# Segment 0 moved into the load phase of a memory-recurrent attention kernel, with batched rows redistributed over the segments

## The chip, the cores and the metric

The kernel runs on one core of one Trainium2 chip. The metric is the device time of an execution in microseconds. Seven runs of the kernel before have a median of 942.41 us (939.52 to 943.75). Below, us are microseconds, PE is TensorE, DVE is VectorE, ACT is ScalarE, POOL is GpSimd, SP is SyncE, which here only issues transfers.

## The reference, cut to what matters

Part A is an attention over segments with a memory: 64 segments of 32 tokens, each preceded by 8 memory rows that are the first 8 output rows of the segment before.

```
for s in range(n_seg):                       # 64 segments, in sequence
    xs = x[:, s*32:(s+1)*32]                 # layer-normed input
    h = concatenate([mem, xs], axis=1)       # 8 + 32 rows
    q, k, v = h@Wq, h@Wk, h@Wv               # 32 heads of 128
    p = softmax(where(mask, q@k.T * scale, -1e9))
    o = (p @ v) @ Wo                         # 40 rows of 512
    mem = o[:, :8];  outs.append(o[:, 8:])
h = x + concatenate(outs)
h2 = h + gmlp(layernorm(h))                  # part B
```

Each segment waits for the one before through `mem`. Of h's 40 rows in a segment, 8 are memory rows and 32 are rows of x, which are known from the start.

## The kernel before, in words

The program is recorded by an `Emitter`: each call of `pe`, `act`, `dve`, `pool`, `sp` appends an instruction to that engine's list, with waits derived from the tokens that it reads and writes. So each engine works in the order in which the Python code calls it, and a call that stands early is executed early on its engine. PE's list is the order of the work. PSUM has 8 banks, which are tokens too.

**What is done per segment and what in batches.** A segment computes 32 of its 40 rows itself: 8 memory rows and the first 24 rows of x (the slot `hT`). The last 8 rows of x of each segment ("x rows" here) are done in batches: a chunk is 16 segments, so 128 rows, gathered by `load_xe`, normalised (`ln_inplace`), transposed (`xT`) and kept in `hTe`. For a chunk, 16 groups `qkx_mm`/`qkx_evac` (L370 to L389; 16 matmuls of 128x128 each, into `QTx`) make their Q and K, and 8 groups `vx_mm`/`vx_evac` (L391 to L410; 16 matmuls on 32 columns with 512 elements each) make their V. V of the batch is staged in the two buffers `Vs`, stored to DRAM (`vext_d`), and read back per segment by `load_vx` (L412) into `Vx`, in another layout. A load of `Vx` needs all 8 groups of its chunk to be stored.

**Load phase (L290 to L709).** SP issues, in order: the rows of chunks 0 and 1, four quarters of Wq, the memory, two blocks of x (which wait until the first buffers are free), four quarters of Wk, of Wv, of Wo, 1 MB each. PE transposes the rows of chunks 0 and 1, does the 16 Q/K groups of chunk 0 (after group 7 it transposes two blocks of x and the memory), then the 8 V groups of chunk 0, and then segment 0. The V groups are stored from ACT's queue. `late_consts` (L303) is a row of 35 small instructions on POOL that builds masks; the reciprocal root of a layer norm (L334, L336) is on POOL too, behind what stands there.

**The loop over segments (L764).** In PE's order: Q and K of both halves (`QK`, L437, 64 matmuls), scores (`S_half`), exponential, V (`V_half`, L531), sums (L497, L502), logarithm (L509), reciprocal by exponential (L513), normalisation on DVE (`sm_norm`, L517, L522), then `PV_half` (L548, L554; the second needs `Vx`), evacuation to `cT` (L567, L569), `Wo` (L581), evacuation to `part` (L593), `mem_out` (L600) and its copy into the next segment's slot (L603), after which the next segment's L437 may begin. Every fourth segment also has `F_group` and `WoX_scatter` (L610, L635) for a finished block of 128 rows, `WoX_mm` (L625) runs in each segment from 4 on.

Into this order are put: one Q/K group of the next chunk in each of segments 0 to 47, between the V matmuls and PV (`gx.pour(16)`, L819), and the V groups of the next chunk in 8 of 16 segments (`VXS`, L745): one atom (4 matmuls) ahead of `Wo`, two ahead of `mem_out`, one behind it (L833, L847, L856). SP issues in each second segment a piece of the transposed w_sp (`wT_piece`, L669: a transposing load, then a store that waits for it).

After the loop stands part B (L876 on), which the change doesn't touch.

Of the kernel before, what the change touches and what calls it, by code (L numbers as in the profile page):

```python
# [33 lines left out]
class Emitter:  # L34
    ENGS = ("pe", "act", "dve", "pool", "sp")

    def __init__(self, n_dma_sems=16):
        self.ops = []
        self.by_eng = {e: [] for e in self.ENGS}
        self.last_w = {}  # L40
        self.readers = {}
        self.n_dma_sems = n_dma_sems
        self.dma_rr = 0
        self.dma_cnt = [0] * n_dma_sems
        self.dma_last = [None] * n_dma_sems
        self.const_tokens = set()
# [4 lines left out]
    def add(self, eng, fn, reads=(), writes=(), dma=False, after=()):  # L51
# [21 lines left out]
        if dma:  # L73
            j = self.dma_rr
            self.dma_rr = (self.dma_rr + 1) % self.n_dma_sems
            op.is_dma = True
            op.dma_sem = j
            self.dma_cnt[j] += 1
            op.dma_val = 16 * self.dma_cnt[j]
            if self.dma_last[j] is not None:  # L80
                deps.add(self.dma_last[j])
            self.dma_last[j] = op
# [78 lines left out]
def fast_path(nc, st, keep, A_x, A_mem0, A_Wq, A_Wk, A_Wv, A_Wo, A_seg_len, B_w_in, B_w_sp, B_b_sp, B_w_out, out):  # L161
# [15 lines left out]
    CK = 16  # L177
# [29 lines left out]
    hTe = sb("hTe", [128, 2, DC, 128], BF)  # L207
# [69 lines left out]
    def load_x(rb, j):  # L277
        sp(lambda e: e.dma_start(xn[:, j, :], xr[:, rb, :]), writes=[("xn", j)])

    def load_xe(ck, j):  # L280
        sp(lambda e: e.dma_start(xn[:, j, :], xe[CK * ck:CK * ck + CK, XM:SEG, :]), writes=[("xn", j)])
# [7 lines left out]

    load_xe(0, 0)  # L290
    load_xe(1, 1)
    for hq in range(4):
        load_w(0, hq)
# [37 lines left out]
    def ln_inplace(j):  # L331
        dve(lambda e: e.bn_stats(out=st1[:, j, :], in_=xn[:, j, :]), reads=[("xn", j)], writes=[("st1", j)])
        dve(lambda e: e.bn_aggr(out=mv1[:, j, :], in_=st1[:, j, :]), reads=[("st1", j)], writes=[("mv1", j)])
        pool(lambda e: e.tensor_scalar(out=rs1[:, j:j + 1], in0=mv1[:, j, 1:2], scalar1=EPS, scalar2=None, op0=ALU.add),  # L334
             reads=[("mv1", j)], writes=[("rs1", j)])
        pool(lambda e: e.tensor_tensor(out=rs1[:, j:j + 1], in0=rs1[:, j:j + 1], in1=mhalf[:, 0:1], op=ALU.pow),  # L336
             reads=[("rs1", j), "mhalf"], writes=[("rs1", j)])
        dve(lambda e: e.tensor_scalar(out=xn[:, j, :], in0=xn[:, j, :], scalar1=mv1[:, j, 0:1], scalar2=rs1[:, j:j + 1],
                                      op0=ALU.subtract, op1=ALU.mult),
            reads=[("xn", j), ("mv1", j), ("rs1", j)], writes=[("xn", j)])  # L340

    def xT(j, bank):
        for dc in range(DC):
            pe(lambda e, dc=dc: e.transpose(out=psb[:, bank, dc * 128:(dc + 1) * 128], in_=xn[:, j, dc * 128:(dc + 1) * 128],
                                            identity=ident[:, :]),
               reads=[("xn", j), "ident"], writes=[PB(bank)])
# [10 lines left out]
    def xe_copy(ck, bank):  # L357
        src = psb[:, bank, 0:512].rearrange("p (dc c) -> p dc c", dc=DC)
        act(lambda e: e.activation(out=hTe[:, ck % 2, :, :], in_=src, func=ACT.Copy), reads=[PB(bank)], writes=[("hTe", ck % 2)])
# [10 lines left out]
    def qkx_mm(ck, i, bank, only_hh=None, only_dc=None):  # L370
        mi, h0 = i // 8, 4 * (i % 8)
        ws = (w_q, w_k)[mi]
        for hh in range(4):
            h = h0 + hh
            for dc in range(DC):
                if only_hh is not None and (hh, dc) != (only_hh, only_dc):
                    continue
                pe(lambda e, h=h, dc=dc, hh=hh: e.matmul(ps[:, bank, hh * 128:(hh + 1) * 128], lhsT=ws[:, dc, h * DH:(h + 1) * DH],  # L378
                                                         rhs=hTe[:, ck % 2, dc, :], start=(dc == 0), stop=(dc == DC - 1)),
                   reads=[("hTe", ck % 2), ("W", mi, h // 8)], writes=[PB(bank)])  # L380
# [10 lines left out]
    def vx_mm(ck, n, bank, only=None):  # L391
        for dc in range(DC):
            if only is not None and dc != only:
                continue
            for c in range(4):
                q = slice(32 * c, 32 * c + 32)
                pe(lambda e, dc=dc, c=c, q=q: e.matmul(ps[q, bank, :], lhsT=hTe[:, ck % 2, dc, q], rhs=w_v[:, dc, n * 512:(n + 1) * 512],  # L397
                                                       start=(dc == 0), stop=(dc == DC - 1), tile_position=(0, 32 * c)),
                   reads=[("hTe", ck % 2), ("W", 2, n // 2)], writes=[PB(bank)])

    def vx_evac(ck, n, bank, eng="act", queue="sp"):
        j = n % 2
        if eng == "act":
            act(lambda e: e.activation(out=Vs[:, j, :], in_=ps[:, bank, :], func=ACT.Copy), reads=[PB(bank)], writes=[("Vs", j)])  # L404
        else:
            dve(lambda e: e.tensor_copy(out=Vs[:, j, :], in_=ps[:, bank, :]), reads=[PB(bank)], writes=[("Vs", j)])
        b, c = n // 4, n % 4
        dst = vext_d[ck, 4 * c:4 * c + 4, :, b * DH:(b + 1) * DH].rearrange("g t e -> t g e")
        em.add(queue, lambda e: e.dma_start(dst, Vs[:, j, :].rearrange("p (g e) -> p g e", g=4)), dma=True, reads=[("Vs", j)],
               writes=[("vext", ck, n)])  # L410

    def load_vx(s):  # L412
        i = s % CK
        sp(lambda e: e.dma_start(Vx[:, s % NVX, :, :], vext_d[s // CK, :, 8 * i:8 * i + 8, :]),
           reads=[("vext", s // CK, n) for n in range(8)], writes=[("Vx", s % NVX)])
# [259 lines left out]
    for j in range(2):  # L675
        ln_inplace(j)
        xT(j, 6 + j)
        xe_copy(j, 6 + j)
    load_x(0, 0)
    load_x(1, 1)  # L680
# [3 lines left out]
    ebank = (0, 1, 2, 3)  # L684

    def start_group(cnt, mm, ev, *a):
        bk = ebank[cnt % 4]
        mm(*a, bk)
        ev(*a, bk, "act" if cnt % 2 == 0 else "dve")

    for i in range(16):
        start_group(i, qkx_mm, qkx_evac, 0, i)
        if i == 7:
            for j in range(2):
                ln_inplace(j)
                xT(j, 6 + j)
                ring_copy(j, 6 + j)
            mem0_transpose(5)
# [6 lines left out]
    for n in range(8):  # L705
        bk = ebank[n % 4]
        vx_mm(0, n, bk)
        vx_evac(0, n, bk, "act" if n % 2 == 0 else "dve", "act")
    for s in range(2):  # L709
        load_vx(s)  # L710
# [20 lines left out]
    gx, gv = Gap(), Gap()  # L731

    def qkx_atoms(ck, i):
        mms = [lambda ck=ck, i=i, hh=hh, dc=dc: qkx_mm(ck, i, XB, hh, dc) for hh in range(4) for dc in range(DC)]
        f = lambda: qkx_evac(ck, i, XB, "dve")
        f.eng = "dve"
        gx.add(XB, mms, f)

    def vx_atoms(ck, n):
        mms = [lambda ck=ck, n=n, dc=dc: vx_mm(ck, n, VXB, dc) for dc in range(DC)]  # L740
        f = lambda: vx_evac(ck, n, VXB, "act")
        f.eng = "act"
        gv.add(VXB, mms, f)

    VXS = (0, 1, 4, 5, 7, 8, 9, 12)  # L745
# [18 lines left out]
    for s in range(NSEG):  # L764
        j4 = s % 4
        rb = s // 4
        ck, i16 = s // CK + 1, s % CK
        if ck < NCK:
            if i16 == 0:
                for n in range(8):  # L770
                    vx_atoms(ck, n)
            qkx_atoms(ck, i16)
# [8 lines left out]
        if i16 == 11 and 2 <= ck + 1 < NCK:  # L781
            load_xe(ck + 1, 1)
# [6 lines left out]
        if s == NSEG - 1:  # L789
            load_wT(0, [lastop["q"]])  # L790
        S_half(s, 0)
        sm_exp(0)
        V_half(s, 0)
# [11 lines left out]
        sm_rcp(0)  # L805
        V_half(s, 1, (0, 1, 2))
# [12 lines left out]
        ev = gx.pour(16)  # L819
        PV_half(s, 0)  # L820
        PV_half(s, 1)
        cT_evac(0, "act")
# [9 lines left out]
        vx = i16 in VXS  # L832
        late = gv.pour(vx)  # L833
# [11 lines left out]
        if i16 == 12 and 2 <= ck + 1 < NCK:  # L845
            ln_inplace(1)
        late += gv.pour(2 * vx)  # L847
# [3 lines left out]
        if i16 == 13 and 2 <= ck + 1 < NCK:  # L851
            xT(1, XB)
            late.append(lambda: xe_copy(ck + 1, XB))
        if s + 1 < NSEG:
            mem_out(s)
        late += gv.pour(vx)  # L856
# [15 lines left out]
    assert not gx.atoms and not gv.atoms  # L872
# [922 lines left out]
```

## Time and profile before

| what | value |
|---|---|
| median of 7 runs | 942.41 us |
| profiled execution, its own time | 942.1 us |
| its span in the trace | 940.4 us |
| PE busy | 882.6 us (94%) |
| DVE, ACT, POOL busy | 445.3, 478.5, 109.0 us |
| chain that ended last | PE 90%, ACT 4%, DVE 2%, DMA 2% |
| first L437 of segment 0 / of segment 1 | 51.37 / 65.19 us |
| last L603 (end of segment 62) | 746.21 us |

How to read it: the span is cut by the profiler at the first and last instruction, the run's own time includes what lies around it. "Busy" of PE is the time in which some matmul is in flight. The chain that ended last is followed back from the last instruction to whatever released each step. The granted clock (PEclk) is the share of full speed that TensorE had. Line numbers are those of the kernel before; after the change they are some 25 higher from L412 on.

### The profile page before, as it was taken

How to read it: one execution, taken by the hardware profiler on the slowest of the kernel's cores; microseconds unless marked ns; L12 is line 12 of the kernel's file. 1: busy time of each engine (PE TensorE's matmuls, PEld its weight loads, DVE VectorE, ACT ScalarE, POOL GpSimd, SP SyncE). 2: the span in 40 equal slices, each digit the busy share in tenths (PEclk: the TensorE clock that was granted, in tenths of full speed). 3: DMA queues.
4: the chain of work that ended last, by engine and by line, in shares of the span. 5: the costliest groups of instructions: out<-in, count | busy, mean ns of one | idle time of the engine just before them, and what ended most of it. 6: DMA issues, size and time to landing. Idle time of an engine off the chain costs nothing.

```text
span 940.4 us, 45489 instructions
## 1 busy us (share of the span) xinstructions
PE 882.6 (94%) x20973; PEld 492.2 (52%) x20973; DVE 445.3 (47%) x1029; ACT 478.5 (51%) x1158; POOL 109.0 (12%) x274
## 2 busy tenths in 40 slices
PE   4789999999999999999999999989899999989998
PEld 4545555555555555555555555445444444434443
DVE  3135445455555445555545455444434463453433
ACT  2146666666666666666666666665556565500000
POOL 5001011011111111111111011111101022200000
PEclk9779999999999999999999999999999999999999
DMA  9942012130222222221212131513122193021201
GB/s 333 376 119 69 17 37 65 49 82 20 63 55 56 46 63 45 46 60 38 60 37 66 43 82 23 113 40 68 48 43 63 43 286 106 1 90 45 90 12 36
DMA packets 103668, 71.29 MB, mean 76 GB/s; under 512 B 62248, under 2 KB 89008, under 8 KB 103472
## 3 DMA queue, kind: packets, MB, share of 16 engines
q1 hardware_dynamic: 99248, 67.27, 25.4%
q8 instruction: 166, 2.72, 1.2%
q10 hardware_dynamic: 4224, 1.05, 0.5%
q14 instruction: 30, 0.25, 0.1%
HBM read 39.46 MB, written 18.61 MB: 62 GB/s over the span
## 4 chain that ended last, share of the span: by engine, by line
PE 90%; ACT 4%; DVE 2%; DMA 2%; issue 2%; POOL 0%; ACTq 0%; POOLq 0%
PE f_ps L437 25%; PE f_ps L581 12%; PE f_ps L531 11%; PE f_ps L938 10%; PE f_ps L378 7%; PE f_ps L625 4%; PE f_ps L900 3%; PE f_ps L548 3%; PE f_ps L931 2%; PE f_ps L1008 2%; PE f_ps L397 2%; PE f_ps L600 2%; PE f_ps L476 2%; DMA vext_d<-f_Vs 2%; ACT f_hT L603 1%
## 5 line engine op out<-in xcount | busy, mean ns | idle before, releaser
L437 PE MATMUL f_ps<-f_arena,f_hT 128*32 128x512 bf16 x4096 | 235.5, 383 | 17.3 <-ACT f_hT L603 12.0
L444 ACT ACTIVATE f_Tst<-f_ps 128x512 bf16<-128x512 f32 x256 | 152.6, 597 | 103.4 <-PE f_ps L437 101.2
L437 PEld LDWEIGHTS f_ps<-f_arena,f_hT 128*32 128x32 bf16 x4096 | 104.5, 97 | 127.9 <-ACT f_hT L603 24.1
L531 PE MATMUL f_ps<-f_arena,f_hT 128*32 128x512 bf16 x2048 | 140.2, 378 | 0.0
L450 DVE STREAM_TRANSPOSE f_QT<-f_Tst 128x256 uint32<-128x256 uint32 x128 | 57.0, 446 | 173.8 <-ACT f_Tst L444 173.8
L581 PE MATMUL f_ps<-f_arena,f_cT 128*32 128x384 bf16 (+1 forms) x4096 | 123.6, 273 | 2.1 <-ACT f_cT L567 1.5
L581 PEld LDWEIGHTS f_ps<-f_arena,f_cT 128*32 128x32 bf16 x4096 | 84.8, 97 | 55.9 <-ACT f_cT L567 26.4
L938 PE MATMUL f_ps<-f_arena 128*128 128x512 bf16 x448 | 101.3, 379 | 2.4 <-DVE f_arena L944 1.6
L593 ACT ACTIVATE f_part<-f_ps 128x384 bf16<-128x384 f32 (+1 forms) x128 | 46.4, 384 | 75.1 <-PE f_ps L581 75.1
L453 DVE STREAM_TRANSPOSE f_KT<-f_Tst 128x256 uint32<-128x256 uint32 x128 | 57.0, 445 | 52.7 <-ACT f_Tst L444 52.6
L460 POOL COPY f_QT<-f_arena 128x256 bf16<-128x256 bf16 x64 | 30.8, 481 | 392.7 <-PE f_ps L482 392.6
L569 DVE TENSOR_SCALAR f_cT<-f_ps 128x320 bf16<-128x320 f32 x128 | 56.9, 486 | 38.1 <-PE f_ps L554 38.1
L938 PEld LDWEIGHTS f_ps<-f_arena 128*128 128x128 bf16 x448 | 43.5, 98 | 55.9 <-DVE f_arena L944 2.6
L378 PE MATMUL f_ps<-f_hTe,f_arena 128*128 128x128 bf16 x1024 | 70.3, 227 | 0.1
L378 PEld LDWEIGHTS f_ps<-f_hTe,f_arena 128*128 128x128 bf16 x1024 | 61.7, 102 | 11.7 <-issue 11.6
L567 ACT ACTIVATE f_cT<-f_ps 128x320 bf16<-128x320 f32 x128 | 49.0, 435 | 34.2 <-PE f_ps L554 34.2
L517 DVE SCALAR_TENSOR_TENSOR f_E_sb<-f_R_sb,f_E_sb 128x160 bf16<-128x160 f32 x128 | 41.7, 325 | 46.5 <-ACT f_R_sb L513 46.5
L509 ACT ACTIVATE f_R_sb<-f_ps 128x160 f32<-128x160 f32 x128 | 39.0, 305 | 35.7 <-PE f_ps L502 35.7
L531 PEld LDWEIGHTS f_ps<-f_arena,f_hT 128*32 128x32 bf16 x2048 | 44.6, 95 | 21.0
L589 POOL COPY f_cTx<-f_cT 128x256 bf16<-128x256 bf16 x64 | 26.2, 410 | 196.5 <-DVE f_cT L569 196.5
L397 PE MATMUL f_ps<-f_arena,f_hTe 128*32 128x512 bf16 x512 | 42.2, 394 | 5.0 <-ACT f_Vs L404 4.9
L944 DVE TENSOR_TENSOR f_arena<-f_ps,f_arena 128x512 f32<-128x512 f32 x28 | 19.3, 691 | 57.8 <-PE f_ps L938 57.8
(95 smaller groups left out, 1083.7 us busy)
## 6 DMA issues: line engine op xcount, KB each, us to landing
wT_d<-f_wst SPq DMA_DIRECT2D x32, 256.0 KB, 2.6
f_arena<-wT_d SPq DMA_DIRECT2D x32, 256.0 KB, 4.7
f_arena<-in_A_Wq_dram SPq DMA_DIRECT2D x4, 1024.0 KB, 9.7
f_arena<-in_A_Wk_dram SPq DMA_DIRECT2D x4, 1024.0 KB, 14.1
f_arena<-in_A_Wv_dram SPq DMA_DIRECT2D x4, 1024.0 KB, 14.4
f_arena<-in_A_Wo_dram SPq DMA_DIRECT2D x4, 1024.0 KB, 14.0
f_Vx<-vext_d SPq DMA_DIRECT2D x64, 64.0 KB, 2.9
vext_d<-f_Vs SPq DMA_DIRECT2D x24, 128.0 KB, 2.0
```

Of the source, the lines that this page charges most:

```text
L378: pe(lambda e, h=h, dc=dc, hh=hh: e.matmul(ps[:, bank, hh * 128:(hh + 1) * 128], lhsT=ws[:, dc, h * DH:(h + 1) * DH], rhs=hTe[:, ck % 2, d ...
L397: pe(lambda e, dc=dc, c=c, q=q: e.matmul(ps[q, bank, :], lhsT=hTe[:, ck % 2, dc, q], rhs=w_v[:, dc, n * 512:(n + 1) * 512], start=(dc == 0 ...
L437: pe(lambda e, dc=dc, c=c, rhs=rhs: e.matmul(ps[32 * c:32 * c + 32, bank, :], lhsT=hT[:, sl, dc, :], rhs=rhs, start=(dc == 0), stop=(dc == ...
L444: act(lambda e: e.activation(out=Tst[:, tb, :].rearrange("p (hp i r) -> p hp i r", i=32, r=2), in_=ps[:, bank, :].rearrange("p (hp r i) -> ...
L450: dve(lambda e: e.transpose(out=dst, in_=src), reads=[("T", tb)], writes=[("QT", b)])
L453: dve(lambda e: e.transpose(out=dst, in_=src), reads=[("T", tb)], writes=[("KT", b)])
L531: pe(lambda e, dc=dc, c=c, c0=c0: e.matmul(ps[32 * c:32 * c + 32, bank, :], lhsT=hT[:, sl, dc, :], rhs=w_v[:, dc, c0:c0 + 512], start=(dc ...
L567: act(lambda e: e.activation(out=dst, in_=src, func=ACT.Copy, scale=UNSC), reads=[PB(PVB[c])], writes=[("cT", c)])
L569: dve(lambda e: e.tensor_scalar(out=dst, in0=src, scalar1=UNSC, scalar2=None, op0=ALU.mult), reads=[PB(PVB[c])], writes=[("cT", c)])
L581: pe(lambda e, h=h, g=g, i=i, b=b, c=c: e.matmul(ps[32 * g:32 * g + 32, bank, 0:d1 - d0], lhsT=cTh[:, i, 8:40], rhs=w_o[:, h, d0:d1], star ...
L593: act(lambda e: e.activation(out=part[:, s % 8, d0:d1], in_=ps[:, bank, 0:d1 - d0], func=ACT.Copy), reads=[PB(bank)], writes=[("part", s % ...
L938: pe(lambda e: e.matmul(ps[:, bank, 0:TB], lhsT=z2[:, sc, fb * 128:(fb + 1) * 128], rhs=wTb[tb % 2][:, :, sc, :], start=(sc == 0), stop=(s ...
```

## The change

1. **Loads.** SP issues: rows of chunk 0, Wq's first quarter, rows of chunk 1, two blocks of x, Wq's second quarter, rows of chunk 2, the rest. The two blocks and the rows of chunk 2 go into tiles of `part` (numbers 4, 5, 6), which are free at that time, instead of waiting for `xn`. `hTe` has three buffers instead of two.
2. **Load phase on PE.** Only chunk 0's rows are normalised and transposed ahead of the first Q/K group. The other four are interleaved with groups 1 to 7. After groups 9, 11, 13 and 15 stands one Q/K group of chunk 1 each.
3. **Segment 0** begins after the Q/K groups. The 8 V groups of chunk 0 and four more Q/K groups of chunk 1 stand inside it. Each V group of chunk 0 is staged in a tile of `part` of its own, `Vs` serves the others in turn.
4. **The Vx loads of segments 0 and 1** are issued by POOL, with two semaphores of their own, after `qx_copy(1)`; before, SP issued them ahead of all other transfers of the loop.
5. **In the loop**, `gx` holds one whole group per segment: the 8 V groups of chunk 1 in segments 0 to 7, then the remaining 8 Q/K groups of chunk 1, then those of chunks 2 and 3. The V groups of chunks 2 and 3 are poured one atom behind `mem_out` in each segment and one ahead of it in segments with s mod 4 of 0 or 1, until they are used up (64 atoms, segments 0 to 42). None stands ahead of `Wo`.

```diff
-    hTe = sb("hTe", [128, 2, DC, 128], BF)
+    hTe = sb("hTe", [128, 3, DC, 128], BF)
...
+    def xbuf(j):
+        return (xn[:, j, :], [("xn", j)]) if j < 2 else (part[:, j, :], [("part", j, 0), ("part", j, 1)])
...
     load_xe(0, 0)
+    load_w(0, 0)
     load_xe(1, 1)
-    for hq in range(4):
+    load_x(0, 4)
+    load_x(1, 5)
+    load_w(0, 1)
+    load_xe(2, 6)
+    for hq in range(2, 4):
         load_w(0, hq)
...
     def vx_evac(ck, n, bank, eng="act", queue="sp"):
-        j = n % 2
+        if ck == 0:
+            t, tok = part[:, n, :], [("part", n, 0), ("part", n, 1)]
+        else:
+            j = vcnt[0] % 2
+            vcnt[0] += 1
+            t, tok = Vs[:, j, :], [("Vs", j)]
...
-    for j in range(2):
-        ln_inplace(j)
-        xT(j, 6 + j)
-        xe_copy(j, 6 + j)
-    load_x(0, 0)
-    load_x(1, 1)
+    ln_inplace(0)
+    xT(0, 6)
+    xe_copy(0, 6)
     for hq in range(4):
         load_w(1, hq)
     late_consts()
-    ebank = (0, 1, 2, 3)
+    ebank = (2, 3, 4, 5)
...
     for i in range(16):
-        start_group(i, qkx_mm, qkx_evac, 0, i)
+        start_x(0, i)
+        if i == 1:
+            ln_inplace(1)
+            ln_inplace(4)
+        if i == 3:
+            xT(1, 7)
+            xe_copy(1, 7)
+            ln_inplace(5)
+            ln_inplace(6)
+        if i == 5:
+            xT(4, 6)
+            ring_copy(0, 6)
+            xT(5, 7)
+            ring_copy(1, 7)
         if i == 7:
-            for j in range(2):
-                ln_inplace(j)
-                xT(j, 6 + j)
-                ring_copy(j, 6 + j)
-            mem0_transpose(5)
+            xT(6, 6)
+            xe_copy(2, 6)
+            mem0_transpose(7)
+        if i >= 9 and i % 2 == 1:
+            start_x(1, i // 2 - 4)
...
-    for n in range(8):
-        bk = ebank[n % 4]
-        vx_mm(0, n, bk)
-        vx_evac(0, n, bk, "act" if n % 2 == 0 else "dve", "act")
-    for s in range(2):
-        load_vx(s)
...
+    for n in range(8):
+        vx_group(1, n)
+    for ck, i0 in ((1, 8), (2, 0), (3, 0)):
+        for i in range(i0, 16):
+            qkx_group(ck, i)
+    for ck in (2, 3):
+        for n in range(8):
+            vx_atoms(ck, n)
...
                 QK_evac(s, b, mi)
...
+        if s == 0:
+            for n in range(2):
+                start_v(n)
         S_half(s, 0)
         sm_exp(0)
+        if s == 0:
+            for n in range(2, 4):
+                start_v(n)
+            start_x(1, 4)
         V_half(s, 0)
...
         sm_rcp(0)
+        if s == 0:
+            for n in range(4, 6):
+                start_v(n)
+            start_x(1, 5)
+            for n in range(6, 8):
+                start_v(n)
         V_half(s, 1, (0, 1, 2))
...
-        ev = gx.pour(16)
+        if s == 0:
+            for j in range(2):
+                load_vx(j, "pool")
+        ev = [gx.pop(0)()] if gx else []
         PV_half(s, 0)
         PV_half(s, 1)
+        if s == 0:
+            for i in range(6, 8):
+                start_x(1, i)
         cT_evac(0, "act")
...
-        vx = i16 in VXS
-        late = gv.pour(vx)
+        late = []
         Wo((0, 2, 1, 3), OB, 0, OC)
...
-        late += gv.pour(2 * vx)
+        if j4 < 2:
+            late += gv.pour(1)
...
         if s + 1 < NSEG:
             mem_out(s)
-        late += gv.pour(vx)
+        late += gv.pour(1)
```

## The prediction

> **What bounds the kernel now.** I read the slices of the page first, then the chain of work that ended last for the start, the busy time by stages, and the same chain for single segments of the steady loop. All of it says: TensorE's order of work sets the end, with a hole at the start.
>
> ```profile
> PEclk9779999999999999999999999999999999999999
> ```
>
> A slice is 23.5 us. In slices 2 and 3 TensorE gets 0.7 of its clock, after that the full one to the end. The chain of the start (start, duration, what):
>
> ```profile
> 35.49 7.81 DMA vext_d<-f_Vs
> 43.39 0.61 ACT f_Vs L404
> 44.02 6.62 DMA vext_d<-f_Vs
> 50.72 0.61 ACT f_Vs L404
> 51.37 3.63 PE f_ps L437 x32
> ```
>
> The reader sees that the batched V rows of chunk 0 have only two staging buffers (Vs), so the third group waits 7.8 us until a store has landed, the fifth 6.6 us more. Segment 0 (its L437) starts at 51.37; the same chain has segment 1's L437 at 65.19. The stages (us, PE busy, PEld, DVE, ACT, POOL, granted clock, DMA share, GB/s):
>
> ```profile
> 23.00:29.00 6.00, 5.72 (x55) 5.51 (x56) 0.92 (x2) 1.18 (x3) 0.08 (x1) 0.50 1.05 387
> 39.00:44.00 5.00, 0.13 (x4) 0.00 (x0) 0.00 (x0) 0.60 (x1) 0.00 (x0) 0.90 1.12 359
> 44.00:57.00 13.00, 9.40 (x92) 2.96 (x96) 2.27 (x4) 2.02 (x4) 0.00 (x0) 0.52 0.73 216
> ```
>
> TensorE idles twice for about 5 us: from 17.8 to 23.3 but for four transposes (0.4 us), and from 39.2 to 44.0. After each its clock stands at 0.50, for about 7 and 13 us. DMA, over 1 in its column, is saturated until about 50.7 us (by stretches of 2 us, 48 to 50 has 1.14, 50 to 52 has 0.37): weights fill it.
>
> Now the steady loop. A segment with a Q/K group of the batched rows (L378) and one without, from the chain:
>
> ```profile
> 175.27 0.21 ACT f_hT L603
> ...
> 181.64 1.00 PE f_ps L378 x16
> ...
> 186.24 0.21 ACT f_hT L603
> ```
>
> ```profile
> 669.83 0.21 ACT f_hT L603
> ...
> 676.04 0.31 ACT f_R_sb L509
> 676.37 0.35 ACT f_R_sb L513
> ...
> 680.74 0.21 ACT f_hT L603
> ```
>
> With the group a segment lasts 10.97 us (186.24 - 175.27), without it 10.91 (680.74 - 669.83): its 1.00 us stands in a hole in which TensorE otherwise waits for logarithm, exponential and normalisation. Batched work in the loop is thus nearly free, and moving it out brings nearly nothing. The exception, a V group on a segment that also has F_group and WoX_scatter:
>
> ```profile
> 141.28 0.22 PE f_ps L610 x4
> 141.50 0.21 PE f_ps L635 x4
> 141.71 0.43 PE f_ps L397 x7
> ...
> 142.33 0.21 ACT f_hT L603
> ```
>
> This segment began at 130.91, so it took 11.42: two fillers of 0.43 each ahead of mem_out don't both fit.
>
> **The change, part by part.** The sum is made against the profiled execution, 942.1 us (span 940.4, 1.7 around it); the median of the runs shown is 942.41, 0.3 above.
>
> *Q/K rows in the load phase.* SP now issues xe0, Wq, xe1, x0, x1 and xe2 without its old wait for the transposes (1.6 us on L278, with DMA full anyway: worth nothing). xe2 adds 128 KB, 0.34 us at 387 GB/s. Four layer norms (blocks 1, 4, 5, 6) are interleaved with groups 1 to 7. Their reciprocal root runs on POOL, behind late_consts: that took from 7.61 to 18.89, 11.3 us; it now starts after one norm, at 5.3, and ends at 16.6. So norm 1 is done at 17.9 (0.9 POOL, 0.4 DVE), and each further one takes 2.3 us (18.46 to 20.77 in the trace): 20.2, evacuation of group 3 on DVE 0.7, then 23.2 and 25.5. TensorE runs in order: after group 3 (about 13.4) it stands at the transpose of block 1 until 17.9, a new idle stretch of 4.5 us. From 26.2 there are 12 groups (8 of chunk 0, 4 of chunk 1) at 0.89 us (the spacing of evacuations from 30.3 to 33.9): segment 0 starts at about 36.9. All Wk has landed by then (last issue 12.99 + 15.5 us to landing, + 0.34 = 28.8). If the idle stretch halves the clock, as the two of before did, it is about 39.5.
>
> *Segment 0 with the V groups in it.* Ahead of its PV stand QK 3.64, eight V groups at 0.87, two Q/K groups at 0.9, V 1.73, scores and sums 0.85, a V group of chunk 1 0.87, and a last wait of 0.8 for the normalisation: 16.6 us, so TensorE is at PV at 53.5 (56.1 with the slow clock). The part tiles give all eight V groups a buffer of their own: the 16.8 and 15.1 us of waits of ACT and DVE for stores go.
>
> *What is late next.* PV needs Vx, Vx needs all eight stores, and these share the DMA engines with Wo. Before, DMA was full until 50.7 with four stores served. Queue q10 (the eight stores) took 7.5% of the engines over 62 us, 0.58 us a store. Four more stores 2.3, xe2 0.34, and wT_piece(0), which SP now issues before the Vx loads rather than after, about 1.4 (256 KB in and out at 387 GB/s): full until 54.7 in all, against the last issue of a store at 51.6 + 2 (its landing time once Wo is out). With the landing the last store is in at about 55.5 (before: 57.7, when SP was released). The stores on ACT's queue cost 8 issues of 0.37 us among ACT's segment work; it hides beside TensorE's V groups.
>
> *The Vx loads on POOL.* No transfer is issued by POOL in the trace. Nearest row below: the same load from SP, 2.2 to 2.9 us to landing. Above: the wait of a 128 KB store behind full rings, 7.8. I take 3.2, by the nearer row (same load, DMA nearly empty): Vx is there at 58.7. The second load waits for the first, and cTx_copy(0) behind it on POOL for both; its first waiter is cT_evac of segment 1, some 8 us later: hidden. For a POOL-issued transfer the Trainium skill ("DMA: Bandwidth & Descriptors", Latency and other measured facts) states about 1 us to the first byte against 0.6 from SP; by that the load would take 0.4 more than SP's, 3.3 at most, and no run here shows it.
>
> *After PV.* Two more Q/K groups (1.8 us) stand ahead of Wo. Their evacuations (0.6 ACT, 0.7 DVE) come before cT_evac on both engines, so Wo's later quarters wait: 0.4 PV, 0.9 + 0.7 to the first two evacuations, 0.9 and 1.0 cT, 1.1 rest of Wo, 0.6 part_evac, 0.5 mem_out and hT: 6.0 us, where before took 3.8 (61.42 to 65.19). Segment 1 starts at 58.7 + 6.0 = 64.7, against 65.19: **-0.5 us**. The 14 us that segment 0 starts earlier are given back, as DMA and not TensorE now sets its middle.
>
> *The clock.* TensorE idles at PV from 53.5 to 58.7, 5 us, as long as the stretch from 39.2 to 44.0 after which the clock halved. That would cost half of some 5 us at half speed, 2.5. In the branch with the slow clock earlier the idle is only 3 us. I count +0.2 for the two together. The Trainium skill ("TensorE: Matmul & The Clock Gate", Part 1) speaks against this change: one idle window of 3.4 us halves the clock; by that rule alone the full 2.5 would stand here, and the forecast would be 2.3 later. The rows agree in kind, but the stretch from 47.8 to 51.4 fell in an already slow clock and can't tell the bound.
>
> *Steady loop.* First L603 of the loop at 64.94, last at 746.21, 62 periods; the last 15 are 10.91. So the 47 before average (681.27 - 163.65)/47 = 11.01. After the change a V group of chunk 1 takes the place of a Q/K group in segments 0 to 7 (same hole, 0.87 for 1.00), and a V atom of 0.22 stands behind mem_out in every segment to 42 (in the 0.27 us hole until hT is there) and one ahead of it where no F_group or transpose stands. No segment then carries 0.86 there, which removes three times 0.45, and the rest goes from 10.99 to about 10.96: 47 x 0.05 = **-2.4 us**. Bounds: 0 and 47 x 0.10 = -4.7.
>
> Sum: 942.1 - 0.5 + 0.2 - 2.4 = **939.4 us**.
>
> **Rivals.** *Overlap works better* (0.17): stores drain early, POOL's load lands in 2.2 us, no clock loss: segment 1 at 62 to 62.7, -2.8, steady -2.7: 936.6. For it: DMA has room from 50.7 on. Against: the eight stores' bytes.
> *The clock halves at PV* (0.20): segment 1 at 66.5, +1.3, steady -2.4: 941.0. For it: both idle stretches of 5 us did so.
> *Fillers pay* (0.08): the atom behind mem_out hides a longer hole than 0.27 in all 43 segments, 0.1 more each: 935. Against: segments with and without V groups differ by 0.04 now.
> *Slower* (0.10): the Vx load on POOL comes late. wT_piece(0)'s transpose and store, now ahead, fill the rings, the last store lands 3.9 later (half of the 7.8 above) at 59.4, POOL's load takes 6 (between 2.9 and 7.8), and the clock halves: 59.4 + 6 + 6.0 + 2.5 = 73.9, 8.7 later, less 2.4: 948. For a time 2.8 above the median segment 1 must start 5.5 later, at 70.7: this decides once Vx lands after 64.7, or after 62.2 with the slow clock. Against: SP's own loads there landed in 2.9.
> That the change doesn't do what it says is excluded in part: the order of instructions puts segment 0's L437 before all V groups, but segment 1 may still start no earlier, which is the second rival.
>
> **Numbers.** Forecast 0.45, half of it on either side of 0.3% (2.8 us, about what a measurement of this kernel can tell from no change). Faster: 0.23 + 0.17 + 0.08 = 0.48; within: 0.22 + 0.17 + 0.03 = 0.42; slower: 0.03 + 0.07 = 0.10. The range leaves out the slow case and most of the filler case: 935.5 to 943.0. The forecast's own range is 938 to 941.
>
> **What would show it.** Right: the first wait for POOL in front of the transpose of block 1; L437 of segment 0 near 37 to 39; a wait of TensorE in PV for Vx's DMA, ended near 59; segment 1 at 64 to 65; segments near 10.96. Wrong: segment 1 before 62 (DMA backlog smaller) or after 67 (POOL's load, clock), or periods of 11.0 or more.

## The result and the profile after

| | before | after |
|---|---|---|
| median of all runs | 941.12 us (50 runs, 939.22 to 944.31) | 944.29 us (19 runs, 942.39 to 946.86) |
| profiled execution, its own time | 942.1 us | 943.16 us |
| its span | 940.4 us | 941.4 us |
| first QK matmul of segment 0 | 51.37 us | 36.95 us |
| first QK matmul of segment 1 | 65.19 us | 68.19 us |
| first to last copy into the next slot (62 periods) | 681.3 us | 679.3 us |
| last copy to the end of the span | 194.2 us | 194.2 us |

The changed kernel is slower: its time is 1.0034 of before's, interval 1.0025 to 1.0043, so some 3.2 us. The pair of profiled executions differs by 1.06 us only: 3.0 us lost at the start, 2.0 won in the loop. The rest is in the executions that were profiled: before's lay 1.0 above its median, after's 1.1 below. A second profile of each (the last two experiments) shows where.

In after's code QK is L462, the batched Q/K groups L396, the batched V groups L415, their copies L427 (ACT) and L429 (DVE), PV L573 and L579, Wo L606, the copy into the next slot L628, the Vx load L439.

The slices of after, clock and DMA. The low clock of before's slices 2 and 3 is gone from this coarse view; what is left of it lies within the first and third slice:

```profile
PEclk8989999999999999999999999999999999999999
DMA  9951312140312111221303120413112193021201
```

The chain of after from the last V groups of chunk 0 to segment 1 (start, duration, what):

```profile
49.46 1.87 PE f_ps L415 x32
...
51.36 0.69 DVE f_part L429
52.05 0.12 DVE f_E_sb L542
52.17 5.43 DMA vext_d<-f_part
57.60 0.03 POOLq L154
57.63 0.55 issue
58.18 2.29 DMA f_Vx<-vext_d
...
61.01 3.54 PE f_ps L396 x32
...
64.57 0.69 DVE f_arena L407
65.26 0.41 DVE f_cT L594
...
65.71 1.61 PE f_ps L606 x56
...
67.94 0.21 ACT f_hT L628
...
68.19 1.90 PE f_ps L462 x29
```

Three things are to be read. The last store is issued at 52.2 and has landed at 57.6. POOL then needs 0.55 us to issue the load and 2.29 until it has landed. Behind PV stand two Q/K groups that take 3.54 us for 32 matmuls, twice their usual time, and Wo's later quarters can't run before the evacuations of these two groups.

The same stretch by stages of after (us, busy PE, PEld, DVE, ACT, POOL, granted clock, DMA share, GB/s):

```profile
18.00:22.00 4.00, 3.77 (x36) 3.77 (x37) 2.75 (x7) 1.19 (x2) 0.88 (x3) 0.50 1.05 388
...
48.00:50.00 2.00, 2.00 (x36) 1.27 (x32) 0.68 (x2) 0.60 (x1) 0.00 (x0) 1.00 1.13 358
50.00:52.00 2.00, 2.00 (x51) 0.94 (x40) 0.84 (x3) 0.60 (x1) 0.00 (x0) 1.00 1.77 251
...
58.00:60.00 2.00, 0.00 (x0) 0.00 (x0) 0.00 (x0) 0.00 (x0) 0.77 (x1) 0.53 0.43 137
60.00:62.00 2.00, 1.48 (x35) 1.41 (x36) 0.00 (x0) 0.00 (x0) 0.53 (x1) 0.50 0.03 8
62.00:64.00 2.00, 2.00 (x21) 2.00 (x20) 0.00 (x0) 1.14 (x3) 0.00 (x0) 0.50 0.13 33
```

From 58.1 to 65.0 the clock is halved, just when TensorE has work again. And DMA: its share adds up the times of all packets, so it can pass 1. From 50 to 52 it is 1.77 for 251 GB/s, where the 2 us before have 1.13 for 358, so a byte takes 2.2 times as long. That is when the transposing load of SP's piece of w_sp has come to its turn (its packets run from 50.3 to 54.3).

What TensorE waited for in the start of after (total, times, longest):

```profile
PE f_ps L579 <- DMA f_Vx<-vext_d: 6.3, 1, 6.3
PE f_ps L362 <- DVE f_xn L356: 3.6, 1, 3.6
```

In the loop, the segment of after that has both a V group and F_group and WoX_scatter (L635, L660), from copy to copy:

```profile
133.44 0.21 ACT f_hT L628
...
139.81 0.86 PE f_ps L415 x16
...
143.90 0.22 PE f_ps L635 x4
144.12 0.21 PE f_ps L660 x3
...
144.54 0.21 ACT f_hT L628
```

It took 11.10 us, where the segment of before that the prediction quotes took 11.42: the V group now stands ahead of PV, and only F_group and WoX_scatter lie ahead of `mem_out`.

### The profile page after: what moved, and what is told of

Read it like the earlier page. It is cut to its first block, busy times and chain, and to the rows that moved or that the text cites. A ratio compares the mean times of both kernels' runs of the same rounds, so it can differ in the third digit from the quotient of the medians.

```text
span 941.4 us, 45485 instructions
## 1 busy us (share of the span) xinstructions
PE 889.1 (94%) x20973; PEld 491.1 (52%) x20973; DVE 447.1 (47%) x1033; ACT 475.8 (51%) x1154; POOL 109.9 (12%) x276
## 4 chain that ended last, share of the span: by engine, by line
PE 90%; ACT 3%; DVE 2%; issue 2%; POOL 1%; DMA 1%; POOLq 0%
PE f_ps L462 25%; PE f_ps L606 12%; PE f_ps L556 11%; PE f_ps L1004 10%; PE f_ps L396 6%; PE f_ps L650 4%; PE f_ps L966 3%; PE f_ps L573 3%; PE f_ps L997 2%; PE f_ps L1074 2%; PE f_ps L625 2%; PE f_ps L415 2%; PE f_ps L501 2%; ACT f_hT L628 1%; PE f_ps L522 1%
## 5 line engine op out<-in xcount | busy, mean ns | idle before, releaser
L462 PE MATMUL f_ps<-f_arena,f_hT 128*32 128x512 bf16 x4096 | 232.8, 380 | 9.5 <-ACT f_hT L628 6.4
L462 PEld LDWEIGHTS f_ps<-f_arena,f_hT 128*32 128x32 bf16 x4096 | 104.9, 97 | 120.5 <-ACT f_hT L628 24.1
L606 PE MATMUL f_ps<-f_arena,f_cT 128*32 128x384 bf16 (+1 forms) x4096 | 124.1, 273 | 2.2 <-ACT f_cT L592 1.6
L606 PEld LDWEIGHTS f_ps<-f_arena,f_cT 128*32 128x32 bf16 x4096 | 83.9, 97 | 60.5 <-ACT f_cT L592 30.7
L396 PE MATMUL f_ps<-f_hTe,f_arena 128*128 128x128 bf16 x1024 | 71.7, 230 | 1.6 <-DMA f_arena<-in_A_Wq_dram 1.6
L396 PEld LDWEIGHTS f_ps<-f_hTe,f_arena 128*128 128x128 bf16 x1024 | 63.3, 104 | 12.7 <-issue 9.5
L573 PE MATMUL f_ps<-f_E_sb,f_V_sb 32*128 32x40 bf16 x2048 | 36.8, 178 | 11.1 <-DVE f_E_sb L547 8.9
L1010 DVE TENSOR_TENSOR f_arena<-f_ps,f_arena 128x512 f32<-128x512 f32 x28 | 19.3, 690 | 57.8 <-PE f_ps L1004 57.8
```

The source lines that it names most:

```text
L462: pe(lambda e, dc=dc, c=c, rhs=rhs: e.matmul(ps[32 * c:32 * c + 32, bank, :], lhsT=hT[:, sl, dc, :], rhs=rhs, start=(dc == 0), stop=(dc == ...
L573: pe(lambda e, q=q, c=c, g=g, c0=c0: e.matmul(ps[:, PVB[c], c0:c0 + 40], lhsT=V_sb[q, b, g * 128:(g + 1) * 128], rhs=E_sb[q, b, g * 40:(g ...
L606: pe(lambda e, h=h, g=g, i=i, b=b, c=c: e.matmul(ps[32 * g:32 * g + 32, bank, 0:d1 - d0], lhsT=cTh[:, i, 8:40], rhs=w_o[:, h, d0:d1], star ...
```

## The experiments

**Theory A**, after the first look: the start of after is set by DMA. The last V store lands late behind Wo and the w_sp piece, then come the load of Vx, the two Q/K groups, and most of it at half the clock since TensorE idled for 6.3 us at PV. Its rivals, each in its run: POOL's path for the load; the row of constants on POOL; TensorE's order; the new pattern in the loop.

In the table, "ratio" is against before on the same chip, and the rest is from each kernel's profiled execution (us; an empty cell was not read out): the first QK matmul of segment 0, the last V store landed, Vx there, segment 1's QK in the chain, the half clock near PV (from the trace's record of the clock), the 62 periods of the loop.

| run | median (runs) | ratio, interval | QK 0 | store | Vx | QK 1 | half clock | loop |
|---|---|---|---|---|---|---|---|---|
| after | 944.29 (19) | 1.0034, 1.0025 to 1.0043 | 36.95 | 57.6 | 60.5 | 68.19 | 58.1 to 65.0 | 679.3 |
| after, again | 943.60 (1) | | | 57.1 | 60.1 | 67.83 | 57.4 to 64.3 | 679.0 |
| before, again | 939.88 (1) | | 49.80 | | | 63.88 | 41.4 to 55.1 | 681.0 |
| w_sp piece later | 941.93 (12) | 1.0008, 0.9996 to 1.0020 | 36.9 | 54.9 | 57.9 | 65.19 | 57.6 to 61.0 | 679.2 |
| fillers ahead of PV | 942.06 (12) | 1.0015, 1.0003 to 1.0027 | 37.0 | 56.8 | 59.7 | 65.38 | 58.9 to 65.8 | 679.6 |
| constants later | 943.00 (12) | 1.0023, 1.0012 to 1.0035 | 34.1 | 55.7 | 58.7 | 66.45 | 53.3 to 63.5 | 679.2 |
| old V pattern | 947.35 (6) | 1.0067, 1.0049 to 1.0084 | 36.9 | 57.8 | 60.7 | 70.56 | 56.0 to 69.6 | 681.0 |
| Vx on SP, w_sp later | 941.32 (12) | 0.9991, 0.9979 to 1.0002 | 36.8 | 55.3 | 57.6 | 65.3 | 55.7 to 62.6 | 679.4 |
| before with 8 staging tiles | 938.30 (6) | 0.9959, 0.9942 to 0.9975 | 41.08 | 53.9 | 56.2 | 62.50 | 55.3 to 62.1 | 681.5 |
| w_sp later, fillers ahead | 940.21 (12) | 0.9982, 0.9970 to 0.9993 | | 55.0 | 57.9 | 63.58 | 57.5 to 64.3 | |
| clock kept | 943.75 (12) | 1.0020, 1.0006 to 1.0033 | | 57.1 | 60.0 | 66.01 | none | |
| V first | 942.26 (12) | 1.0002, 0.9989 to 1.0015 | 43.9 | | | 65.79 | 49.6 to 56.4 | 678.9 |
| V first, constants later | 938.52 (10) | 0.9970, 0.9953 to 0.9986 | 41.58 | | | 60.89 | none | 679.2 |

**1. The w_sp piece later.** After with one edit: the first piece goes to segment 1, behind the Vx loads on SP's queue.

```diff
-        if s % 2 == 0 and s // 2 < NWT:
+        if s % 2 == 0 and 0 < s // 2 < NWT:
             wT_piece(s // 2)
+        if s == 1:
+            wT_piece(0)
```

> One part undone: the first piece of the transposed w_sp (a transposing load and a store of 256 KB) is issued by SP in segment 1 instead of ahead of segment 0. Theory A (the start is set by the DMA engines: loads, then eight stores, then the Vx load, and TensorE waits at PV): the last V store lands about 2 us earlier, near 55.5 in place of 57.6, Vx near 58.4 in place of 60.5, segment 1 starts near 66.0 in place of 68.2, time 2 us under the changed kernel. Rival B (the piece is hidden, the stores are late because their packets are slow): stores and segment 1 within 0.5 us of where they were.

The chain of this run:

```profile
51.98 2.90 DMA vext_d<-f_part
...
55.47 2.40 DMA f_Vx<-vext_d
...
65.19 3.64 PE f_ps L462 x64
```

The last store waits 2.90 us instead of 5.43, with its issue at the same time, and segment 1 starts 3.0 us earlier; by the ratios the time falls by 2.4 us (0.0026 of 941). The same piece stands ahead in five profiles (after twice, fillers, old pattern, clock kept: landed at 56.8 to 57.8, mean 57.3) and behind in three (this one, Vx on SP, both together: 54.9 to 55.3, mean 55.1). So it costs the last store 2.2 us, 1.5 to 2.9. (In "constants later" the piece is ahead as well, but the store is issued 3 us earlier.) Of the 3.0 us of segment 1, 2.6 are the earlier Vx and 0.4 the half clock, which was shorter in this profile.

**2. The fillers ahead of PV.** After with the two Q/K groups moved from behind PV to ahead of it, so that they run while Vx is awaited.

```diff
-        PV_half(s, 0)
-        PV_half(s, 1)
         if s == 0:
             for i in range(6, 8):
                 start_x(1, i)
+        PV_half(s, 0)
+        PV_half(s, 1)
```

> The last two Q/K groups of segment 0 stand ahead of PV instead of behind it; nothing else is moved. Theory A: TensorE is idle there anyway (54 to 60.5), so the groups cost nothing in that place, and behind PV the 3.6 us that they took at half clock and the delay of their evacuations go: segment 1 starts 2.5 to 3.5 us earlier, near 65, whether the clock still halves or not; time 2.5 to 3.5 us under the changed kernel. Rival (the two groups were beside other waits behind PV): less than 1 us.

Its chain:

```profile
52.42 4.36 DMA vext_d<-f_part
...
60.75 3.61 PE f_ps L606 x64
...
65.38 3.72 PE f_ps L462 x34
```

From Vx (59.72) to segment 1 it is 5.7 us instead of 7.7, so the two groups cost 2.0 behind PV, and nothing ahead of it. In time it is 1.8 us by the ratios, less than the 2.5 to 3.5 expected; their intervals overlap a little. The clock was halved all the same: Wo's 64 matmuls took 3.61 us, 1.92 in the steady loop.

**3. The constants later.** After with POOL's row of 35 instructions behind the layer norms.

```diff
-    late_consts()
...
             mem0_transpose(7)
+            late_consts()
```

> The row of mask constants on POOL is recorded behind the layer norms of the load phase, so the norms no longer wait for it. The stall of TensorE at the transpose of block 1 (14.5 to 18.2) goes and segment 0 starts near 32 in place of 37. Theory A (DMA sets the start): the V stores are issued 5 us earlier but share the engines with Wo for longer, the last one lands within 1.5 us of 57.6, segment 1 starts within 2 us of 68.2, no gain. Rival D (the stall behind the constants sets the start): segment 1 starts 4 to 5 us earlier, time 4 to 5 us under the changed kernel.

The last store in its chain:

```profile
49.07 6.65 DMA vext_d<-f_part
```

Segment 0 starts 2.9 us earlier (5 were expected), segment 1 only 1.7. After has 52.17 and 5.43 in this line: the store is issued 3.1 us earlier and lands 1.9 earlier. So of what TensorE wins, the part that DMA lets through arrives; in time it is 1.0 us by the ratios, whose intervals overlap, and the 4 to 5 us of the rival are not there.

**4. The old V pattern in the loop.** After with `VXS` and its pours of before for the V groups of chunks 2 and 3 (the V groups of chunk 1 stay ahead of PV).

```diff
+    VXS = (0, 1, 4, 5, 7, 8, 9, 12)
...
-        late = []
+        vx = s % CK in VXS
+        late = gv.pour(vx)
...
-        if j4 < 2:
-            late += gv.pour(1)
+        late += gv.pour(2 * vx)
...
-        late += gv.pour(1)
+        late += gv.pour(vx)
```

> Startup as changed, but the V atoms of chunks 2 and 3 are poured in the old pattern (8 of 16 segments, one atom ahead of Wo, two ahead of mem_out, one behind). My theory of the loop: the even spread is worth about 2 us from segment 1 to the end; with the old pattern the stretch from segment 1 to the end is about 1 to 1.5 us longer than in the changed kernel (16 segments instead of the former 24 carry groups, two of them with 0.45 too much), the start is the same. Rival (the spread itself costs time and the old pattern was better): 1 us or more shorter.

The loop takes 681.0 us, 1.7 more than after's profile and as much as before's. So the spread of the V groups makes nearly all of the 2.0 us that the loop gained. That the start is 2.4 us longer as well was not expected: one V atom then stands ahead of segment 0's Wo, and the clock stayed halved for 13.7 us. How much of the 2.4 is the atom and how much the clock was not separated.

**5. The Vx loads on SP.** Experiment 1 with `load_vx(j)` in place of `load_vx(j, "pool")`.

> As the kernel with the w_sp piece issued in segment 1, and the Vx loads of segments 0 and 1 issued by SP instead of POOL. Theory A: the load from POOL took 2.4 us after 0.55 us until its issue; from SP the same load took 2.2 to 2.9 in the kernel before, so Vx lands within 0.6 us of 57.9 and the time is within 1 us of that kernel. Rival C (the load on POOL is the slow step): segment 1 starts 2 us or more earlier.

The load of this run, from the wait's end to its landing:

```profile
55.31 0.02 issue
55.33 2.25 DMA f_Vx<-vext_d
```

On SP it is 2.3 us, on POOL (experiment 1) 0.03 + 0.55 + 2.40, so 3.0: POOL's path costs 0.7 us (the 0.4 that the prediction quotes for it is too little). But the two profiles reach segment 1 within 0.1 us of each other, as here the store landed 0.4 later and the clock was halved for longer. The ratios, 1.0008 and 0.9991, have intervals that overlap. The load on POOL is not what made the change slow.

**6. Before with eight staging tiles.** The kernel before, in which the V groups of chunk 0 get a tile of `part` each; nothing else of the change.

```diff
+        t, tok = Vs[:, j, :], [("Vs", j)]
+        if ck == 0:
+            t, tok = part[:, n, :], [("part", n, 0), ("part", n, 1)]
...
```

The copies and the store behind it use `t` and `tok` in place of `Vs`.

> The kernel before, with one edit alone: each V group of chunk 0 gets a staging tile of its own (part). The V groups run from 34 to 41 without waiting for stores and segment 0 starts near 41 instead of 51.4. Theory A (the engines of DMA, not the staging, hold the start): the last store lands near 54 instead of 57.7, Vx near 57, TensorE waits 7 us at PV and its clock halves; segment 1 starts near 62.5, 2 to 3 us earlier than in the kernel before, time 2 to 3 us under it. Rival E (staging was the gate): segment 1 starts near 55, time 9 to 10 us under the kernel before.

Its chain (L440 is QK here):

```profile
43.75 10.12 DMA vext_d<-f_part
...
53.88 2.33 DMA f_Vx<-vext_d
...
62.50 3.64 PE f_ps L440 x64
```

This is the kernel with the lowest median of the study: 0.9959 of before, and 0.9925 of after if the two ratios are divided (0.9959 / 1.0034). It has none of the early segment 0 and none of the new loop (681.5 us), yet segment 1 starts at 62.50, 5.7 us before after's. The V groups stand ahead of segment 0, so their stores are queued while Wo still flows; the last one waits 10 us, but beside segment 0's work, and has landed at 53.9. The rival, with segment 1 at 55, fell: a transfer again ends the wait. At PV TensorE waits 2.9 us for it, not the 7 expected, since it has stood 2.4 us earlier for ACT, which was held in the issue of the stores (up to 2.06 us for one).

**7. Both edits, 1 and 2, in one kernel.**

> The changed kernel with both mends: the w_sp piece in segment 1, and the last two Q/K groups ahead of PV. Theory A: Vx near 57.9, TensorE idle for 2.5 to 3 us only, so its clock mostly stays full; segment 1 starts near 62, time 5 to 7 us under the changed kernel and 2 to 4 us under the kernel before. Rival (each mend takes away the same wait): no more than 3 us under the changed kernel.

Segment 1 at 63.58, 4.6 us earlier than after; 4.9 us by the ratios. One by one the two edits brought segment 1 forward by 3.0 and 2.8 (0.8 of the second was a store that landed earlier in that profile), so they nearly add up. The half clock stays, from 57.5, though TensorE waits only 2.7 us for Vx (55.26 to 57.96), and segment 1 misses the expected 62. With these two moves the change makes the kernel a little faster than before (interval 0.9970 to 0.9993).

**8. The clock kept.** After with 96 more matmuls (a Q/K group six times) ahead of PV in segment 0, into a bank whose content is not used, to keep TensorE busy while it waits.

```diff
+        if s == 0:
+            for _ in range(6):
+                qkx_mm(1, 6, 4)
         PV_half(s, 0)
```

> The changed kernel with 96 matmuls more: six times the matmuls of one Q/K group, into a bank that nobody reads in between, ahead of PV of segment 0, where TensorE waits for Vx. The output is the same. Theory A: they fit into the wait (5.4 of 6.4 us), the clock stays full, and the groups and Wo behind PV run at full speed: segment 1 starts 1.5 to 2.5 us earlier than in the changed kernel, near 66, time 1.5 to 2.5 us under it although more is computed. Rival (the clock has no part in it): no gain, or up to 1 us more.

Its chain, and a stage behind PV:

```profile
57.63 2.36 DMA f_Vx<-vext_d
...
60.46 1.91 PE f_ps L396 x32
...
66.01 2.99 PE f_ps L462 x51
```

```profile
60.00:62.00 2.00, 1.96 (x53) 1.92 (x54) 0.00 (x0) 0.50 (x2) 0.53 (x1) 1.00 0.13 33
```

The same 32 matmuls take 1.91 us instead of 3.54, with more work on TensorE and Vx as late as ever (59.99). From Vx to segment 1 it is 6.0 us, in after 7.7: the half clock costs 1.7 us there. In time it is 1.3 by the ratios, whose intervals overlap at their ends; the point rests on the profile.

**9. V first.** After with the V groups ahead of segment 0 as in before, the four Q/K groups of chunk 1 ahead of PV, the w_sp piece later and Vx on SP.

```diff
+    for n in range(8):
+        start_v(n)
...
+        if s == 0:
+            for i in range(4, 8):
+                start_x(1, i)
         ev = [gx.pop(0)()] if gx else []
...
```

The calls of `start_v` and `start_x` that after has inside segment 0 are taken out; the w_sp piece and the Vx loads stand as in experiments 1 and 5.

> Meant to beat both kernels. The changed kernel with: the eight V groups of chunk 0 ahead of segment 0 again (with their eight staging tiles), the four remaining Q/K groups of chunk 1 ahead of PV of segment 0, the w_sp piece in segment 1, the Vx loads on SP. Theory A: V stores issued from 38 to 45, the last lands near 54.5 (DMA full until then, as in the staged kernel before), Vx near 57; TensorE is busy until about 55, so its clock stays full; segment 1 starts near 61, and the loop keeps the 1.8 us of the even spread: time 5 to 6 us under the kernel before (ratio 0.994 to 0.995) and 2 us under the staged kernel before. Rival: the load phase of the change costs what the spread gives, ratio 0.996 as for the staged kernel before.

Neither came out: the time is that of before. Its chain, then two of its stages:

```profile
44.83 1.32 ACTq L432
...
46.82 1.74 ACTq L432
...
48.60 1.66 ACTq L432
...
50.30 1.09 ACT f_Tst L469 x2
```

```profile
48.00:50.00 2.00, 0.00 (x0) 0.00 (x0) 0.00 (x0) 0.00 (x0) 0.00 (x0) 0.89 1.14 362
50.00:52.00 2.00, 0.45 (x12) 0.19 (x16) 0.89 (x2) 1.61 (x4) 0.00 (x0) 0.50 1.16 346
```

TensorE no longer waits for Vx. But ACT, which issues the stores (L432), stands up to 1.74 us in one issue while DMA is saturated, so its first evacuation of segment 0's Q/K comes at 50.30; TensorE waits 3.4 us for it at the scores, and the clock halves. So V first alone brings nothing here: experiment 7, with the V groups inside segment 0, is if anything faster (0.9982 against 1.0002; the intervals just overlap).

**10. V first, constants later.** Experiment 9 with the edit of experiment 3.

> The same with the mask constants behind the layer norms, so the V groups begin 3 us earlier. Theory A (DMA holds Vx): the last store lands within 1 us of the run without this edit, and the time is within 1 us of it. Rival D (the norms hold the start): 2 to 3 us less.

```profile
25.02 14.70 DMA f_arena<-in_A_Wv_dram
...
39.86 1.94 PE f_ps L415 x32
...
44.85 2.28 ACTq L432
...
47.18 1.09 ACT f_Tst L469 x2
...
60.89 3.64 PE f_ps L462 x64
```

That is its chain. Segment 0 starts 2.3 us earlier than in experiment 9, ACT's first evacuation 3.1, and the clock stays whole (no half clock from 22.9 us to 930.9), so segment 1 starts at 60.89, 4.9 before experiment 9's, and the time falls by 3.0 us by the ratios. Theory A had expected little of this edit, as in experiment 3. It falls here, and the rival holds: once Vx is there in time, the constants on POOL, ACT's queue and the clock set the start. In this run DMA does again: the last V groups wait for Wv, which lands at 39.7. The full clock is in part luck: TensorE still waits 2.6 us at the scores (45.22 to 47.83; the last section says why it didn't halve), and the profiled execution is the fastest of the ten (935.83). This kernel (0.9970 of before) and that of experiment 6 (0.9959) both beat before and after; their intervals overlap.

**11 and 12. Both kernels again, one profile each.**

> The changed kernel once more, for a second trace of another execution. Of the 21 executions listed for it the span falls by 0.5 us for each 0.001 of granted clock, so I expect the start of segment 1 to differ from 68.2 by what the clock stands at half speed more or less behind PV, and the loop from segment 1 to the end to be within 0.5 us of 679.3. Rival: the loop differs, the start doesn't.

> The kernel before once more, for a second trace. Its profiled execution (span 940.4) lay above most others; I expect segment 1 to start 1 to 2 us ahead of 65.2, because the half clock after the V groups ends one window earlier, and the loop within 0.5 us of 681.3. Rival: the loop differs, the start doesn't.

After again is like the first profile: last store landed 57.1, half clock 57.4 to 64.3, loop 679.0; only its end after the last copy is longer, 195.3 against 194.2. Before again is not: its segment 0 starts at 49.80 (51.37 in the first profile) and segment 1 at 63.88 (65.19), and it ends 193.5 us after the last copy (194.2). The loop is the same within 0.3 us. The half clock after the V groups is as long in both (13.65 us), not shorter as expected; all of it comes earlier. So before's start varies by more than a microsecond between two executions, and the profile that the prediction was worked from is the later one. The end, which no edit touches, varies too: from 193.3 to 196.6 us over the fourteen profiles, the two longest (experiments 7 and 9) with a piece of half clock at about 833 us.

## Why the prediction was wrong

It gave 939.4 us and a faster kernel as likeliest. The profiled execution of after took 943.16. Two steps failed: the landing of the last V store, put 2.1 us too early, and the clock at PV, put at +0.2 where half speed cost 1.7. The prediction's own sum, 55.5 + 3.2 + 6.0 = 64.7 for segment 1, can be set beside 57.6 + 2.9 + 7.7 = 68.2.

- **"The last store is in at about 55.5"**: wrong by 2.1 us, at 57.6. Experiment 1 divides the miss. The w_sp piece was priced at 1.4 us, by its bytes; it costs the last store 2.2. Without the piece the sum gave 54.1, the runs 55.1, so the other work on the queues was priced 1.0 too low as well (which part of it is not shown); the last 0.3 is this profile's own. The row that shows why bytes were the wrong measure is the stage from 50 to 52: a share of 1.77 for 251 GB/s. The Trainium skill ("DMA: Bandwidth & Descriptors", Why small descriptors are slow) states 27% of overhead for descriptors of 256 bytes (11 cycles for 8 of data), the size of the packets of the piece's load in the trace; its store has 2048. By it alone the piece would be an estimate of 0.9 + 0.7 = 1.6 us. The trace's direction agrees, its size is larger.
- **"I take 3.2"** for POOL's load: 2.9, so 0.3 too much.
- **"6.0 us" from Vx to segment 1, and "I count +0.2" for the clock**: the first right at full clock (experiment 8: 59.99 to 66.01; its listed parts add up to 6.1), the second wrong. The half clock stood through the whole stretch and cost 1.7. The prediction saw that both stretches of 5 us in before had halved the clock, and then took a value near nothing. The rule it quoted from the Trainium skill ("TensorE: Matmul & The Clock Gate", Part 1) and put aside would have been the better term: 2.5, where 1.7 was measured. The second rival, the clock that halves at PV, is what happened; its 66.5 for segment 1 lacks only the late store. The last rival, "slower", had named the piece of w_sp, with 3.9 us for its delay (2.2) and 6 for POOL's load (2.9).
- **The steady loop, -2.4 us**: measured -2.0, within the bounds. The three segments that carried two fillers ahead of `mem_out` gave 0.32, 0.49 and 0.49 us, predicted 0.45 each; the rest gave 0.7. Experiment 4 shows that it is the spread of the V groups.
- **Segment 0 at about 36.9 us** (36.95), **norm 1 at 17.9** (18.2), **TensorE at PV at 53.5** (53.1 to 54.0): right. In the first there is luck: the stall at the transpose of block 1 did halve the clock, from 17.2 to 24.0, for which the prediction had 39.5. It cost nothing, as TensorE was held by the layer norms until 26.2 in any case. "The 14 us that segment 0 starts earlier are given back" was right too, and too kind: they are given back, and 3 us more.
- **The base.** With four terms put right (store, POOL's load, clock, loop) the sum is 939.4 + 2.1 - 0.3 + 1.5 + 0.4 = 943.1, the profiled execution of after. That the medians differ by 3.2 rather than 1.1 is a second error: the sum stood on one execution of before that lay 1.0 above the median of 50 runs, and the seven runs shown hid that (942.41).

**Where the expected gain went.** The wait of ACT and DVE for two staging buffers is gone, and experiment 6 shows that this alone is worth 0.4%. After lies 7.1 us above that kernel by the ratios. Experiment 7 takes 4.9 of them away: the piece of w_sp and the two groups behind PV. In after the last store is issued later than in experiment 6 (its wait begins at 52.2 against 43.8) and lands 3.7 us later (57.6 against 53.9); 2.2 of these are the piece of w_sp. That the rest comes from the order, segment 0's work being used up before the landing that it could have covered, is argued and not shown: experiment 9 put the V groups first again and gained nothing by itself.

**What stays open.** Experiment 8's profiled execution took 941.49, its median is 2.3 us above. The granted clock of its twelve executions is 0.993 to 0.998 (mean 0.9956), that of after's 21 is 0.989 to 0.996 (0.9914), so half clock was rarer in it, but a mean doesn't say where. In experiment 4 the atom and the clock are not separated. Of the piece of w_sp it is the transposing load that delays the store: its own store is issued only at 56.67, and its first packet moves at 57.5, when the last V store is all but in.

## What to carry to other kernels

When a phase is bounded by a saturated DMA, look first at what is issued ahead of the last transfer of the longest chain, and move it behind (the piece of w_sp, 2.4 us); then lay the free work of TensorE into the wait, ahead of the waiting instruction and not behind it (1.8 us). Price a transfer in a saturated stretch by the time that its packets take, and count an idle stretch of TensorE twice: once as waiting, and again as half speed for what follows, where it leaves TensorE busy for less than about half of a piece of 3.41 us (last section). And before a sum is built on one execution, see how far the start varies between executions, since 1 us there was a third of this verdict.

## What the runs showed of the hardware that was not expected

- **Half the clock comes in pieces of 3.41 us**, in the trace's record: 3.41 in experiment 1 (57.57 to 60.98), 6.8 in after (58.14 to 64.96), 10.2 in experiment 3, 13.7 in experiment 4. Within a trace all changes of the clock lie whole pieces apart. The Trainium skill ("TensorE: Matmul & The Clock Gate", Part 1) describes a free-running window of about 3.4 us; the pieces agree with it.
- **What counts is how long TensorE was busy within one piece.** In the fourteen traces the clock halved only behind pieces with at most 1.59 us of work, and came back only behind pieces with 2.81 or more; half clock went on behind pieces with up to 2.67, full clock behind pieces with 1.58 or more (1.58 and 1.59 thus occur on both sides). Where the page gives one idle window for the first and one busy window for the second, these are the measured bounds. Four pieces, from experiment 6 (the clock halves behind it), 10 (it stays full), 4 (it stays halved) and after (it comes back):

```profile
51.88:55.29 3.41, 1.59 (x46) 1.14 (x36) 0.46 (x2) 1.13 (x3) 0.00 (x0) 1.00 0.14 35
...
46.83:50.25 3.42, 1.74 (x76) 1.11 (x80) 1.93 (x5) 2.47 (x6) 0.00 (x0) 1.00 1.13 361
...
62.82:66.23 3.41, 2.63 (x27) 2.08 (x28) 1.40 (x4) 1.25 (x3) 0.00 (x0) 0.50 0.01 1
...
20.59:24.00 3.41, 2.81 (x27) 2.54 (x26) 2.35 (x6) 1.16 (x3) 0.79 (x2) 0.50 1.05 386
```

- **So the price of a gap depends on where it falls.** In experiment 10 a wait of 2.4 us at a transpose (16.59 to 19.02) halved the clock, and one of 2.6 us at the scores didn't, as it lay across two pieces with 1.80 and 1.74 us of work. The gaps at PV in experiments 1 and 5 are 4.1 and 3.7 us; the half clock lasts 3.4 in the one and 6.8 in the other, as its first piece had 3.06 us of work in the one and 1.51 in the other. That is 1.7 us of price by the phase.
- **An engine stands in the issue of a store while DMA is saturated**: ACT 1.3 to 1.7 us for one issue in experiment 9 and up to 2.28 in experiment 10, which the prediction had counted as 0.37 each.
- **The landing of a 128 KB store ranges from 2 to 10 us** by what is queued: 1.95 us for a late one in before's second profile, 2.90 in experiment 1, 10.12 in experiment 6.
